# One normalisation moved to VectorE, one key tile fewer for VectorE, three accumulator banks in the tail of an attention-plus-MLP block on one core

## The chip, the cores and the metric

The kernel runs on one core of one Trainium2 chip. The metric is the device time of one execution in microseconds, and several executions of one kernel are summed up by their median. The profiled execution has a time of its own and a span, from its first to its last instruction. The engines are TensorE (PE; its weight loads are PEld), VectorE (DVE), ScalarE (ACT), GpSimd (POOL) and SyncE (SP), which issues most DMAs.

## The reference, cut to what matters

```python
mod = (_silu(c) @ w_mod).reshape(c.shape[0], 6, 1, -1)
sa, ca, ga, sb, cb, gb = mod[:, 0..5]
h = _layernorm(x) * (1 + ca) + sa                     # x: 2048 tokens x 512
q, k, v = split(h @ wqkv)                             # 32 heads of 16
p = softmax(q @ k.T / 4); o = p @ v
x = x + ga * (o @ wo)
h = _layernorm(x) * (1 + cb) + sb
x = x + gb * (gelu(h @ w1 + b1) @ w2 + b2)            # 512 -> 1376 -> 512
```

## The kernel before

**Attention.** The 2048 queries are four blocks of 512. The heads are worked in 32 groups `qi` of four; the 2048 keys are 16 tiles of 128. For a group and a key tile TensorE makes four 128x512 score tiles (line 944), one for each row `r` of four heads. Two ways lead from the scores to probabilities:

- ScalarE takes the exponential of two score tiles at a time out of PSUM into `pA` or `pB` (line 1300).
- VectorE turns scores into 16-bit integers that, read as half floats, are a rough power of two (line 1371, four passes for one group and key tile). Three shifted copies of the result follow, made by VectorE (line 1342) or GpSimd (line 1348), and TensorE weights the four copies with `VE` and three scaled variants `VV`.

TensorE multiplies the probabilities with the values (line 1108). The key tiles that VectorE may take are listed in `DKT`. In the last query block the last four groups are "halved": each covers four head pairs for 256 tokens, so that the first 256 tokens (the first half) are done with attention earlier than the second half, and one line-1108 product becomes two of 256 columns.

**Order.** A planner runs while the program is built: it simulates the engines with fixed costs and appends instructions to each engine's queue in the simulated order. The engines then run their queues in order, with semaphores. `d_next` decides when VectorE opens a new key tile; in the last group it opens none when fewer than `D_END` of the group's key tiles are unclaimed ("row tiles left"). Tasks such as the norm have an engine, and for the planner a cost.

**The first half.** When its attention is done, `add_half` puts out: the product with `W_o` and the residual (line 789, VectorE), the layer norm's statistics (lines 281, 286, VectorE), the root `ln_root` (lines 291, 292, GpSimd), the norm `n2` (line 804, two tiles of 128 tokens, on the engine that `N2_ENG` names), and two DMA transposes into `ha` (line 513, on SP's queue behind the eight `rb` loads of line 1474). A task of GpSimd can carry a further dependency, by which it starts after the VectorE instruction that preceded it in the plan.

**The tail.** `last_tail` is written by hand and comes after the last group's products. Its own chain is the second half's: copy the accumulator (`o`, line 1639), pick out the denominators (line 1644, fp32 products), reciprocal and spreading (lines 1646 to 1651), normalise (line 1655), `W_z` product, statistics, root on GpSimd, norm on VectorE and ScalarE (lines 1671, 1670), transposes (line 1676), and up products of the second half. Between these steps stands work of the first half, drawn by `gap(n)` from the generator `fillers`: eleven `up_one` (four 128x256 products of `ha` into a PSUM bank, then a gelu on ScalarE, line 1620), each followed by two yields, and then 22 products of the second MLP matrix, eleven for each of two token tiles, into the banks `dA[0]` and `dA[1]`. `GAPS` says how many yields each gap takes.

At the end VectorE adds the residual to the two first-half tiles (`out_add`, line 1690) and then makes `range_flag` (lines 1712 to 1720), a check on the denominators. Its result `bad` is an operand of a 1x1 TensorE product (line 1696), behind which the last 33 MLP products of the second half are queued.

Of the kernel before, what the change touches and what calls it, by code (L numbers as in the profile page):

```python
# [52 lines left out]
PE, AC, DV, PO = range(4)  # L53
# [44 lines left out]
TIE = True  # L98
SEARCH = None
NARROW = False  # L100
GAPS = (4, 2, 2, 17, 2, 3)
NHQ = 4
N2_ENG = PO
NHC = NC - NHQ // 2
MMH = 0.25
SP_DH = (0.5, 1.75)
# [1 line left out]
U2_GATE = (1.7, 4.6)  # L108
OUT2_GATE = (4.6, 7.2)
LOAD_AT = (0, 3)  # L110
D_END = 5
BULK_LEFT = 8
Z_GATE = 0.6

# [49 lines left out]
def adaln_block(ctx: ExitStack, tc: tile.TileContext, A_x, A_wqkv, A_wo, B_x, B_w1, B_b1, B_w2, B_b2,  # L164
# [81 lines left out]
    def bank(i):  # L246
        return PS[:, i, :]
# [41 lines left out]
    def ln_root(mv, n):  # L289
        rs = small.tile([P, 4], FP32, name="rs")  # L290
        nc.gpsimd.tensor_scalar(out=rs[:, 0:n], in0=mv[:, 0:n, 1], scalar1=EPS, scalar2=None, op0=ALU.add)  # L291
        nc.gpsimd.tensor_tensor(out=rs[:, 0:n], in0=rs[:, 0:n], in1=mhalf[:, 0:n], op=ALU.pow)
        return rs
# [36 lines left out]
    def copy(eng, dst, src):  # L330
        if eng == AC:
            nc.scalar.copy(out=dst, in_=src)
        else:
            nc.vector.tensor_copy(out=dst, in_=src)
# [150 lines left out]
    def task(*a, **k):  # L485
        tasks.append(Task(*a, **k))
# [201 lines left out]
    def plain(ps, lhsT, rhs, start, stop):  # L688
        nc.tensor.matmul(out=ps, lhsT=lhsT, rhs=rhs, start=start, stop=stop)  # L689

    def up_mm(ps, h2, fc, j, cs=slice(0, 512), mm=plain):
        mm(ps, late["W_1"][:, j, fc * P:(fc + 1) * P], h2[:, j, cs], j == 0, j == NC - 1)
# [91 lines left out]
    def add_half():  # L784
# [16 lines left out]
        def n2(tt):  # L801
            hn.append(otp.tile([P, 512], BF16, name="OT"))
            eng = nc.vector if N2_ENG == DV else nc.gpsimd
            eng.tensor_scalar(out=hn[tt], in0=xa[:, tt, :], scalar1=XL["mv"][:, tt, 0:1],  # L804
                                    scalar2=XL["rs"][:, tt:tt + 1], op0=ALU.subtract, op1=ALU.mult)

        for tt in range(2):
            task(("n2", b, tt), XA_AT, [("r2", b)] + [("n2", b, 0)] * tt, N2_ENG, 0.36 if N2_ENG == DV else 0.55,
                 lambda tt=tt: n2(tt))
# [8 lines left out]
    def ua(fc):  # L818
        return hT[:, fc // 3, 768 + 256 * (fc % 3):1024 + 256 * (fc % 3)]
# [147 lines left out]
    def d_next(now, avoid):  # L967
        if dcur[0] is None:
# [5 lines left out]
            left = sum(1 for i in range(st["ap"], len(order)) if order[i] not in owner) if aq >= NQ - 1 else 99  # L974
            if left < D_END:
                return None
# [625 lines left out]
    def last_tail():  # L1602
# [13 lines left out]
        def up_one(fc, k, half):  # L1616
            ps = bank(k)[:, 0:256]
            for j in range(NC):
                up_mm(ps, h2 if half else ha, fc, j, hB if half else hA)
            nc.scalar.activation(out=uG[:, fc, hB] if half else ua(fc), in_=ps, func=ACT.Gelu_apprx_tanh, bias=b1c[:, fc:fc + 1],  # L1620
                                 scale=1.0)

        def fillers():
            for fc in range(NFC):
                up_one(fc, (kw, dA[1])[fc % 2], 0)
                for _ in range(2):
                    yield
            for tt in range(2):
                for fc in range(NFC):
                    plain(bank(dA[tt]), ua(fc)[:, tt * P:(tt + 1) * P], late["W_2"][:, fc, :], fc == 0, fc == NFC - 1)  # L1630
                    yield

        gen = fillers()

        def gap(n):
            for _ in range(n):
                next(gen, None)

        nc.vector.tensor_copy(out=o, in_=bank(kO))
        nc.scalar.activation(out=onec, in_=onec, func=ACT.Gelu_apprx_tanh)  # L1640
        gap(GAPS[0])
        cols = [slice(P * i, P * i + P) for i in range(4)]
# [3 lines left out]
        nc.vector.reciprocal(out=rt.rearrange("p t r -> p (t r)"), in_=bank(kd)[:, 0:16])  # L1646
        gap(GAPS[1])
        for i in (0, 2, 1, 3):
            nc.vector.tensor_copy(out=rx[:, cols[i]].rearrange("p (r e) -> p r e", e=32),
                                  in_=rt[:, i, :].unsqueeze(2).to_broadcast([P, 4, 32]))  # L1650
            nc.tensor.matmul(out=bank(kr)[:, cols[i]], lhsT=rx[:, cols[i]], rhs=ident32, start=True, stop=True)
        gap(GAPS[2])
        for t in range(2):
# [10 lines left out]
        rs = ln_root(mv, 2)  # L1664
        gap(GAPS[3])
        nb = small.tile([P, 2], FP32, name="nb")
# [12 lines left out]
        copy(DV, h2[:, 2:4, hB], both[1][:, 2:4, :])  # L1679
        gap(GAPS[4])  # L1680
        for t in range(2):
            copy(DV, xr[:, 2 + t, :], bank(pz[t]))
        for fc in range(NFC):
            up_one(fc, (kO, kw, kd, kr)[fc % 4], 1)
            if fc == GAPS[5]:
                gap(99)

        def out_add(tt, k):
            obs[tt] = tl2.tile([P, D], BF16, name="ob")
# [138 lines left out]

    scr_d1 = scr.tile([4, 512], FP32, name="d1")
    last_tail()  # L1830
    att.close()
    general_path()
# [35 lines left out]
```

## Time and profile before

| what | value |
|---|---|
| median of 3 runs | 761.46 us (759.64 to 761.6) |
| the profiled execution's own time | 760.97 us |
| its span | 759.2 us |
| mean granted TensorE clock | 0.991 |
| busy: PE, ACT, DVE, POOL | 97%, 95%, 90%, 56% |
| last ScalarE exponential starts | 719.46 us |
| last TensorE instruction group starts | 754.35 us |

All times inside the profile are microseconds from the start of the span. The page's second part cuts the span into 40 slices of 19 us; each digit is tenths. The chain of waits names, for the work that ended last, what released each step. "x28" stands for 28 instructions of one kind in a row; their starts are real, and ends of matmuls are modelled, so neighbours overlap by a fraction of a microsecond. In the windows view, PEclk is the TensorE clock that was granted, as a share of full speed.

### The profile page before, as it was taken

The numbers are of one execution on the slowest core, as the hardware profiler recorded it, in microseconds if no ns is written. First come the engines' busy times: TensorE is split into PE (matmuls) and PEld (weight loads), VectorE is DVE, ScalarE is ACT, GpSimd is POOL, SyncE is SP. The second block draws the span as 40 slices with busy tenths as digits, with TensorE's granted clock in tenths as the row PEclk, the third lists the DMA queues.
The fourth block names the chain that finished last, engine by engine and source line by source line (L and its number), as shares of the span: only waits on it lengthen the run. The fifth ranks groups of instructions, "written<-read, shape, count | busy, mean of one in ns | idle before, by whom it ended". The sixth has DMA issues, their size and how long they took to land.

```text
span 759.2 us, 22066 instructions
## 1 busy us (share of the span) xinstructions
PE 737.3 (97%) x9027; PEld 241.3 (32%) x9030; DVE 679.7 (90%) x1189; ACT 719.7 (95%) x777; POOL 421.7 (56%) x266
## 2 busy tenths in 40 slices
PE   7999999999999999999999999999999999999977
PEld 3322322232333222222222222222222223344445
DVE  5958999999999899899999999999999989898823
ACT  3999999999999999999999999999999999999933
POOL 3202556566675655766565667756666465355720
PEclk9999999999999999999999999999999999999979
DMA  9410100021110110000101100000100200011000
GB/s 317 112 18 2 25 10 17 7 91 38 44 50 10 30 24 19 6 21 22 44 17 24 31 10 17 11 15 24 46 16 10 44 8 16 7 41 31 26 16 31
DMA packets 41964, 25.60 MB, mean 34 GB/s; under 512 B 26705, under 2 KB 37010, under 8 KB 41858
## 3 DMA queue, kind: packets, MB, share of 16 engines
q1 hardware_dynamic: 41042, 23.02, 11.7%
q8 instruction: 72, 1.18, 0.6%
q10 hardware_dynamic: 816, 1.12, 0.4%
q14 instruction: 34, 0.28, 0.1%
HBM read 16.59 MB, written 2.61 MB: 25 GB/s over the span
## 4 chain that ended last, share of the span: by engine, by line
PE 44%; ACT 43%; issue 8%; POOL 2%; DVE 1%; DMA 1%; POOLq 0%; ACTq 0%
ACT pB L1300 21%; ACT pA L1300 21%; PE PS L1108 15%; PE PS L944 15%; PE PS L254 10%; PE PS L689 2%; ACT uG L749 1%; POOL t L1348 1%; POOL OT L804 1%; DMA xb<-in_A_x_dram 0%; DVE st L281 0%; PE PS L1125 0%; DVE t L1371 0%; ACT uG L1620 0%; ACT L1300 0%
## 5 line engine op out<-in xcount | busy, mean ns | idle before, releaser
L1348 POOL TENSOR_SCALAR t<-t 128x2048 int16<-128x2048 int16 x188 | 355.7, 1901 | 257.6 <-DVE t L1342 149.7
L1300 ACT ACTIVATE pA<-PS 128x1024 bf16<-128x1024 f32 x368 | 395.1, 1074 | 3.4 <-PE PS L944 3.3
L1300 ACT ACTIVATE pB<-PS 128x1024 bf16<-128x1024 f32 x368 | 395.2, 1074 | 0.2
L1371 DVE TENSOR_SCALAR t<-PS 128x512 int16<-128x512 f32 x576 | 372.6, 682 | 25.0 <-PE PS L944 21.0
L944 PE MATMUL PS<-qm,kT 32*128 32x512 bf16 x2048 | 306.8, 383 | 6.5 <-ACT pA L1300 2.7
L1108 PE MATMUL PS<-t,VV 128*32 128x512 f16 (+1 forms) x1968 | 228.6, 358 | 2.5 <-POOL t L1348 1.4
L944 PEld LDWEIGHTS <-kT 32*128 32x128 bf16 x2048 | 85.1, 91 | 288.6 <-issue 285.5
L1342 DVE TENSOR_SCALAR t<-t 128x2048 int16<-128x2048 int16 x244 | 174.2, 743 | 0.5
L1108 PE MATMUL PS<-pA,VE 128*32 128x512 bf16 (+1 forms) x824 | 170.2, 362 | 0.0
L1108 PE MATMUL PS<-pB,VE 128*32 128x512 bf16 (+1 forms) x824 | 165.7, 362 | 0.0
L1108 PE MATMUL PS<-t,VE 128*32 128x512 f16 (+1 forms) x656 | 134.6, 358 | 0.2 <-DVE t L1371 0.2
L1108 PEld LDWEIGHTS <-VE 128*32 128x32 bf16 x2304 | 70.0, 94 | 76.6 <-issue 70.3
L1108 PEld LDWEIGHTS <-VV 128*32 128x32 bf16 x1968 | 65.4, 95 | 55.6 <-issue 51.1
L254 PE MATMUL PS<-h2T,W 128*32 128x512 bf16 x528 | 42.7, 383 | 0.0
L254 PE MATMUL PS<-W,uG 128*32 128x512 bf16 x528 | 41.3, 383 | 0.0
L1125 PE MATMUL PS<-kT,zeros 128*32 128x512 bf16 x284 | 27.4, 383 | 0.0
L341 DVE TENSOR_SCALAR qm<-PS,qmask 128x512 bf16<-128x512 f32 x32 | 22.5, 743 | 4.6 <-PE PS L254 4.6
L740 DVE TENSOR_SCALAR uG<-PS,b1c 128x512 bf16<-128x512 f32 x33 | 24.5, 744 | 1.1 <-PE PS L254 1.1
L291 POOL TENSOR_SCALAR rs<-mv 128x4 f32<-128x4 f32 (+1 forms) x10 | 4.3, 433 | 37.4 <-DVE mv L286 37.3
L1486 POOL TENSOR_TENSOR OT<-o_sb,rb 128x512 bf16<-128x512 f32 (+1 forms) x17 | 20.0, 1179 | 9.0 <-DVE t L1342 7.6
L254 PE MATMUL PS<-hT,W_k 128*32 128x512 bf16 x256 | 21.3, 394 | 0.9 <-DVE hT L324 0.9
L254 PE MATMUL PS<-hT,W_q 128*32 128x512 bf16 x256 | 21.4, 399 | 0.0
(142 smaller groups left out, 385.2 us busy)
## 6 DMA issues: line engine op xcount, KB each, us to landing
rb<-d SPq DMA_DIRECT2D x112, 32.0 KB
W_m<-in_w_mod_dram SPq DMA_DIRECT2D x2, 1024.0 KB
out_dram<-ob SPq DMA_DIRECT2D x15, 128.0 KB
o_sb<-o SPq DMA_DIRECT2D x56, 32.0 KB
xb<-in_A_x_dram SPq DMA_DIRECT2D x3, 512.0 KB
xr<-in_A_x_dram SPq DMA_DIRECT2D x3, 512.0 KB
W<-in_B_w_dram SPq DMA_DIRECT2D x4, 344.0 KB
W<-in_B_w_dram SPq DMA_DIRECT2D x5, 256.0 KB
```

What stands on the lines that cost most here:

```text
L254: nc.tensor.matmul(out=ps[32 * g:32 * g + 32, :], lhsT=lhsT[:, 32 * g:32 * g + 32], rhs=rhs, start=start, stop=stop)
L341: nc.vector.tensor_scalar(out=qm[(b, ch)][:, par, :], in0=ps, scalar1=qmask[:, par:par + 1], scalar2=None, op0=ALU.mult)
L689: nc.tensor.matmul(out=ps, lhsT=lhsT, rhs=rhs, start=start, stop=stop)
L740: nc.vector.tensor_scalar(out=X["u"][:, fc, :], in0=bank(ps), scalar1=late["b1c"][:, fc:fc + 1], scalar2=None, op0=ALU.add)
L944: nc.tensor.matmul(out=dst, lhsT=kT[rows, ch, kt * P:(kt + 1) * P], rhs=rhs, start=True, stop=True)
L1108: nc.tensor.matmul(out=bank(O[qi])[32 * r:32 * r + 32, cs], lhsT=w, rhs=rhs[:, cs], start=(n == 1 and not halved(qi)), stop=last and (pr = ...
L1125: nc.tensor.matmul(out=bank(O[qi])[32 * r:32 * r + 32, :], lhsT=zeros[:, 0:32], rhs=kT[:, 0, 0:512], start=False, stop=False)
L1300: nc.scalar.activation(out=t[:, 0:n, :], in_=PS[:, b0:b0 + n, :], func=ACT.Exp, scale=math.log(2.0) / STEP)
L1342: nc.vector.tensor_scalar(out=t16[:, rs, :], in0=d["tile"][:, rs, :], scalar1=float(MJ[j]), scalar2=None, op0=ALU.add)
L1348: nc.gpsimd.tensor_scalar(out=t16[:, rs, :], in0=d["tile"][:, rs, :], scalar1=1.0, scalar2=float(MJ[j]), op0=ALU.mult, op1=ALU.add)
L1371: nc.vector.tensor_scalar(out=d["tile"][:, r:r + n, :], in0=PS[:, i:i + n, :], scalar1=T_BIAS, scalar2=0.0, op0=ALU.add, op1=ALU.max)
L1486: nc.gpsimd.tensor_tensor(out=ot[:, 0:w], in0=o[:, 0:w], in1=rb[:, 0:w], op=ALU.mult)
```

## The change

`N2_ENG` becomes VectorE, so the two `n2` tiles run there. `D_END` becomes 6: VectorE opens no new key tile in the last group once fewer than six are unclaimed. The first half's up products rotate over three banks in place of two. And the last gap, which emptied the generator behind the fourth up product of the second half, now takes 13 yields there; what is left comes behind the eleventh.

```diff
-GAPS = (4, 2, 2, 17, 2, 3)
+GAPS = (4, 2, 2, 17, 2, 3, 13)
-N2_ENG = PO
+N2_ENG = DV
-D_END = 5
+D_END = 6
...
         def fillers():
             for fc in range(NFC):
-                up_one(fc, (kw, dA[1])[fc % 2], 0)
+                up_one(fc, (kw, dA[1], dA[0])[fc % 3], 0)
                 for _ in range(2):
                     yield
...
         for fc in range(NFC):
             up_one(fc, (kO, kw, kd, kr)[fc % 4], 1)
             if fc == GAPS[5]:
-                gap(99)
+                gap(GAPS[6])
+        gap(99)
```

The lines behind the change are one line further down in the changed kernel (line 1690 becomes 1691, and so on).

## The prediction

> **What bounds the kernel now.** The page comes first. Its row of the granted clock has full speed everywhere but in one slice, the last but one:
>
> ```profile
> PEclk9999999999999999999999999999999999999979
> ```
>
> So the 720 us ahead of the tail are steady, and the tail is read by itself. The order of instructions in the changed program is that of before up to about 711 us, so all that can change lies behind that point. The chain of waits over the last 39 us:
>
> ```profile
> 720.17 4.15 POOL OT L804 x2
> ...
> 724.33 2.43 DMA hT<-OT
> ...
> 726.80 1.89 PE PS L689 x8
> 728.69 1.50 PE PS L1644 x8
> 730.19 0.87 PE PS L689 x4
> 731.07 1.99 PE PS L1651 x8
> 733.05 2.92 PE PS L689 x12
> ...
> 736.00 0.48 ACT hT L1620
> ...
> 737.16 0.48 ACT hT L1620
> ...
> 739.85 0.78 ACT OT L1670
> ...
> 741.69 6.03 PE PS L689 x37
> ```
>
> GpSimd's two norms (line 804) and the transposes behind them end last, then the tail runs on TensorE, with ScalarE's gelus between. The view of who waited for whom prices the head of this chain, and TensorE's timeline shows what stood before it:
>
> ```profile
> PE PS L689 <- DMA hT<-OT: 4.3, 1, 4.3
> ```
>
> ```profile
> 722.11 0.40 PE L1108 MATMUL PS<-pB,VE 128*32 128x256 bf16 x4
> ```
>
> TensorE ended attention at 722.5 and stood 4.3 us until the first half's `ha` had landed. The price is more than 4.3 us, as the windows show. The columns are: the stretch, its length, busy us of PE, PEld, DVE, ACT and POOL, granted clock, DMA share and GB/s. The cuts lie on one grid of 3.41 us, placed so that each stretch has a single clock:
>
> ```profile
> 8.25:11.66 3.41, 2.23 (x48) 1.71 (x48) 1.67 (x6) 0.83 (x2) 0.68 (x3) 1.00 1.09 350
> 11.66:15.08 3.42, 3.17 (x32) 1.30 (x28) 1.05 (x10) 1.20 (x2) 0.00 (x0) 0.50 1.09 348
> ...
> 721.63:725.04 3.41, 0.88 (x7) 0.17 (x5) 0.69 (x1) 0.47 (x2) 2.67 (x2) 1.00 0.20 38
> 725.04:728.45 3.41, 1.65 (x8) 1.22 (x9) 0.00 (x0) 0.47 (x1) 0.00 (x0) 0.50 0.21 41
> 728.45:731.87 3.42, 3.42 (x18) 2.91 (x17) 0.89 (x5) 0.95 (x2) 0.00 (x0) 0.50 0.02 2
> 731.87:735.29 3.42, 3.42 (x14) 1.95 (x14) 1.23 (x3) 0.47 (x1) 0.00 (x0) 0.50 0.00 0
> ```
>
> The clock was halved behind each window in which TensorE did little, and came back behind a window of dense products. Because of the wait, the tail ran at half clock until 735.29.
>
> **Part 1, the norm on VectorE.** It removes the two GpSimd norms of the chain (4.15 us) and their place behind another GpSimd task. What they need stands in VectorE's and GpSimd's timelines, and what one costs on VectorE in the same operation on the same shape at line 296:
>
> ```profile
> 711.12 0.67 DVE L789 TENSOR_TENSOR hT<-PS,hT 128x512 bf16<-128x512 f32 x1
> ...
> 715.07 4.28 DVE L1342 TENSOR_SCALAR t<-t 128x2048 int16<-128x2048 int16 x7
> ```
>
> ```profile
> 715.24 1.13 POOL L291 TENSOR_SCALAR rs<-mv 128x2 f32<-128x2 f32 x1 [0.64 <-DVE mv L286]
> 716.46 1.12 POOL L292 TENSOR_TENSOR rs<-rs,mhalf 128x2 f32<-128x2 f32 x1
> ```
>
> ```profile
> L296 DVE TENSOR_SCALAR uG<-xr,mv,rs x12: 327/411/415, 260.2 to 588.5; 128x512 bf16<-128x512 bf16 x12
> ```
>
> In the new order VectorE does, after line 789 (done 711.8), the second statistics, one shift and the two aggregates (no passes of a last key tile stand between any more; two and a half steps at the shifts' 4.28 / 7 = 0.61, so by 713.3), then three shifts, the first norm, one shift, the second norm. GpSimd's root takes 2.3 us beside VectorE's shifts, so it is ready by 715.6, and the second norm is done by 715.6 + 0.41 + 0.61 + 0.41 = 717.0. On VectorE the norms queue ahead of the copy of line 1639 alone, which waits for TensorE anyway. SP is at the eight `rb` loads until 716.3:
>
> ```profile
> 712.12 4.20 SPq L1474 DMA_DIRECT2D rb<-d x8
> ```
>
> Before, the landing came 2.4 us after the second norm (724.33 to 726.76). So `ha` lands near 719.5, or 721 with everything as slow as before (root at 717.6). Either is ahead of the end of attention: the wait goes to nothing, and what is late next is attention itself.
>
> **Part 2, one key tile fewer for VectorE.** Four passes and three shifts leave VectorE and GpSimd, 24 products leave TensorE (four filling ones come in), and ScalarE gets two more exponentials, which are the bound there:
>
> ```profile
> 718.56 1.12 ACT L1300 ACTIVATE pA<-PS 128x1024 bf16<-128x1024 f32 x1
> 719.46 1.13 ACT L1300 ACTIVATE pB<-PS 128x1024 bf16<-128x1024 f32 x1
> 720.61 1.28 ACT L1640 ACT_TABLE_LOAD   x1
> ```
>
> Starts are 0.90 apart, so the last ends at 720.59 + 1.80 = 722.4. The last four products follow (0.40 and a semaphore): TensorE is at the tail at 722.9, 0.4 later than before. The fewer products on TensorE (0 to 0.8 us) I take at 0, since ScalarE ends last. The table load now ends at 723.7, beside TensorE's first fillers. So the restart moves from 726.80 to 722.9: **-3.9 us**.
>
> **The clock that comes with it.** With no wait, the clock stays full if the tail's first microseconds count as busy. Four rows then halve: 1.89, 1.50, 1.99 and the `W_z` products,
>
> ```profile
> 733.74 1.78 PE L689 MATMUL PS<-W_z,OT 128*128 128x512 bf16 x4
> 735.36 4.08 PE L689 MATMUL PS<-hT,W 128*128 128x256 bf16 x28
> ```
>
> 7.16 / 2 = 3.6; a little of it turns into waiting for VectorE's steps between them. I take **-3.4 us**, between 0 (clock halved as before) and -3.6.
>
> **Part 3, three banks.** With two banks two gelus took 1.16 us (736.00 to 737.16), since the product waits until the gelu of two before has read its bank. With three the bound is ScalarE, 0.45 each:
>
> ```profile
> 742.33 1.79 ACT L1620 ACTIVATE uG<-PS,b1c 128x256 bf16<-128x256 f32 x4 [0.69 <-PE PS L689]
> ```
>
> Before, line 1670 came 4.49 us after the seven products' start at 735.36 (739.85). Now it is 0.64 for the first product and seven gelus of 0.44: 3.7. That is **-0.75 us**, between 0 and -1.0. Bank `dA[0]` is later the first MLP accumulator; its gelu is two before the last and done by then.
>
> **Part 4, the split gap.** The 17 MLP products before become 13, and four move behind the 28 up products. In TensorE's time that is nothing. But the second `out_add` waits for the last of them, `range_flag` is queued behind it on VectorE, and TensorE's next instruction waits for `bad`. Before, 28 up products hid that:
>
> ```profile
> 743.44 3.83 PE L689 MATMUL PS<-W,hT 128*128 128x512 bf16 x17
> 747.11 3.22 PE L689 MATMUL PS<-h2T,W 128*128 128x256 bf16 x28
> 750.45 0.16 PE L1696 MATMUL PS<-onec,bad 128*1 128x1 bf16 x1
> 750.77 0.59 PE L689 MATMUL PS<-W,uG 128*128 128x512 bf16 x2 [0.16 <-issue]
> ```
>
> ```profile
> 747.30 0.69 DVE L1690 TENSOR_TENSOR ob<-PS,hT 128x512 bf16<-128x512 f32 x1 [1.68 <-PE PS L689]
> ...
> 749.92 0.06 DVE L1720 MEMSET onec<- 128x1 bf16 x1
> ```
>
> From the last MLP product (its end modelled at 747.27) to `onec` done (749.98) are 2.71 us, and from there to the first product behind line 1696 0.79. With nothing left to cover it TensorE stands 3.50 us where it stood 0.44: **+3.1 us**.
>
> The sum against this execution's own 760.97: -3.9 - 3.4 - 0.75 + 3.1 = -4.95, that is 756.0. Then the clock once more: 3.5 us of standing fill most of a 3.41 us window wherever the grid lies. The window 721.63 to 725.04 had 0.88 busy and was followed by half clock, so I take one such window as likely. The rest of the run is 5.0 us of TensorE work, by a last row of the chain:
>
> ```profile
> 750.77 4.96 PE PS L689 x34
> ```
>
> One halved window of dense work, like that from 11.66 to 15.08, costs at most 1.7, less what is still standing: **+1.55**. Bounds are 0 and +5.0 (halved to the end). Forecast: 757.5. The three runs shown have their median 0.5 above the profiled execution and spread over 2 us; I leave the forecast at the profiled level.
>
> **A rule beside this.** The window from 8.25 to 11.66 had 2.23 us of busy time, in small products, and half clock followed. The Trainium skill ("TensorE: Matmul & The Clock Gate", Part 1) states that the free-running window is about 3.4 us and that the clock falls after at least one idle window. If "idle" means wholly idle, the rule would hardly let the clock fall in a 3.5 us wait, and it would be the first rival below; these rows speak against that reading.
>
> **The rivals.**
> First, the clock holds through the flag's wait: 756.0. For it: a stand of 3.50 us can lie astride two windows of 3.41, each then about half busy. Against it: the row with 0.88 busy. Chance 0.25.
> Second, the tail's first microseconds, with the small products of line 1644 and pauses for VectorE, count as idle too. One halved window there costs half of 3.41, 757.5 + 1.7 = 759.2; two cost 760.9. For it: the row 8.25 to 11.66. Against it: by the halved rows 2.1 of the first 3.4 us are wide products (0.95 and 0.44 of fillers, most of 1.0 of line 1651). Chance 0.11, about no change.
> Third, slower, by one mechanism, the clock gate: only windows busy by more than about two thirds count. Then the chain gets none of the 3.4, and after the flag's wait the clock stays halved to the end: 760.97 - 3.9 - 0.75 + 3.1 + 5.0 = 764.4. Against it: the clock came back after one window at 15.08. Chance 0.07.
> Fourth, the change doesn't bring `ha` forward: GpSimd's root starves beside VectorE's shifts, and the restart stays at 726.80. Then nothing pays but the banks: 760.97 - 0.75 + 3.1 + 1.55 = 764.9. The norm would have to be 5 us later than worked out; the root's two rows show 2.3 us beside seven shifts. Chance 0.05.
>
> **How the numbers follow.** The forecast has 0.52, its own range being 756.2 to 758.9. No change is what lies within 0.3%, 2.3 us, about what a measurement of this kernel can tell from none. The forecast but 0.04, and the first rival, are faster: 0.73. That 0.04 and the second rival are the same: 0.15. The third and fourth are slower: 0.12. The range reaches from the first rival with its banks' and chain's far bounds (less 1.0, and 0.5 for the restart: 754.5) to the second rival's far end, 761.0; it leaves out about 0.14.
>
> **What would show it.** In the profile after: line 804 on VectorE near 716, `ha` landed before 720; the last exponential near 721.3; TensorE at the fillers near 723 with full clock; gelus 0.45 apart; line 1670's activation near 732; TensorE standing about 3.5 us ahead of line 1697, released by VectorE, and half clock for up to 3.4 us behind it. It is wrong if TensorE does not stand there, if the restart is not before 724, or if the clock falls between 723 and 732.

## The result and the profile after

The changed kernel takes 756.35 us (median of four runs, 755.61 to 757.42) against 761.51 us of the kernel before (759.64 to 761.6). The ratio is 0.9939, its 95% interval 0.9918 to 0.9961: faster by about 5 us. The profiled execution took 755.64 us, with a span of 753.9 us and a mean granted clock of 0.997. The page's row of the granted clock has its one weak slice at the very end now, no longer one before it:

```profile
PEclk9999999999999999999999999999999999999998
```

The timelines of the changed kernel answer the prediction's steps; the columns are start, length, engine, line, operation, and in brackets the idle time in front and what ended it. First VectorE with the norm (line 804), which waits for GpSimd's root, and SP with the issue of the two transposes that land `ha`:

```profile
711.92 1.86 DVE L1342 TENSOR_SCALAR t<-t 128x2048 int16<-128x2048 int16 x3
714.39 0.41 DVE L804 TENSOR_SCALAR OT<-hT,mv,rs 128x512 bf16<-128x512 bf16 x1 [0.61 <-POOL rs L292]
714.72 0.69 DVE L1342 TENSOR_SCALAR t<-t 128x2048 int16<-128x2048 int16 x1
715.33 0.41 DVE L804 TENSOR_SCALAR OT<-hT,mv,rs 128x512 bf16<-128x512 bf16 x1
```

```profile
714.88 3.63 SPq L513 DMA_TRANSPOSE hT<-OT  x2
```

This row is the issue in SP's queue, and the transfers land later: before, the same row ended at 722.26 + 3.26 = 725.52 and `ha` landed at 726.76. Here the semaphore of the second transpose is complete at 719.64 in the trace, nearly two microseconds ahead of TensorE's need. TensorE's timeline in the tail shows that it no longer waits for `ha`, and where it waits instead:

```profile
721.26 0.29 PE L1108 MATMUL PS<-pB,VE 128*32 128x256 bf16 x2
721.48 1.05 PE L689 MATMUL PS<-hT,W 128*128 128x256 bf16 x8
...
726.77 3.22 PE L689 MATMUL PS<-hT,W 128*128 128x256 bf16 x28
...
736.79 3.22 PE L689 MATMUL PS<-h2T,W 128*128 128x256 bf16 x28
739.85 1.03 PE L689 MATMUL PS<-W,hT 128*128 128x512 bf16 x4
743.65 0.16 PE L1697 MATMUL PS<-onec,bad 128*1 128x1 bf16 x1 [2.78 <-DVE onec L1721]
743.75 3.94 PE L689 MATMUL PS<-W,uG 128*128 128x512 bf16 x11
```

VectorE, in the same stretch, starts the second `out_add` when the last of the four products is done, and the range check stands in its queue behind it:

```profile
740.91 0.69 DVE L1691 TENSOR_TENSOR ob<-PS,hT 128x512 bf16<-128x512 f32 x1 [4.74 <-PE PS L689]
741.52 0.42 DVE L1713 TENSOR_SCALAR rb<-dall 128x512 f32<-128x512 f32 x1
...
743.52 0.06 DVE L1721 MEMSET onec<- 128x1 bf16 x1
```

The view of who waited for whom has at its head the new wait, where it had the one for the DMA before:

```profile
PE PS L1697 <- DVE onec L1721: 2.8, 1, 2.8
```

The windows (columns as in the prediction) say what the clock made of that wait, and that the start of the run has no halved window this time; from 11.66 to 15.08 it had one before. But for the first, they lie on this execution's grid:

```profile
11.66:15.08 3.42, 2.51 (x41) 1.05 (x40) 2.29 (x12) 1.41 (x3) 0.00 (x0) 1.00 1.09 348
...
722.71:726.12 3.41, 2.95 (x24) 2.22 (x24) 1.59 (x7) 1.43 (x4) 0.00 (x0) 1.00 0.03 5
...
739.80:743.21 3.41, 1.07 (x6) 0.33 (x4) 2.23 (x4) 0.72 (x2) 0.00 (x0) 1.00 0.11 38
743.21:746.62 3.41, 2.97 (x8) 1.11 (x9) 0.48 (x4) 0.00 (x0) 0.00 (x0) 0.50 0.00 0
746.62:750.03 3.41, 3.41 (x28) 2.64 (x27) 1.12 (x2) 0.00 (x0) 0.00 (x0) 1.00 0.13 43
```

Because of that first row every later time of the two traces is shifted. The MLP gelu of line 749, long before anything that the change touches, measures the shift; the chain of waits of before, then that of after:

```profile
650.01 4.90 ACT uG L749
```

```profile
648.61 4.90 ACT uG L749
```

That is 1.40 us, in no part of the change. With it taken off, TensorE restarts at 721.48 + 1.40 = 722.88 on the scale of before, where it restarted at 726.80. So two numbers sum up a kernel from here on: the **restart**, TensorE's first filler on the scale of before (by line 749), and the **tail**, from that filler to the end of the span. Before: 726.80 and 759.2 - 726.80 = 32.40. After: 722.88 and 753.9 - 721.48 = 32.42. The restart came 3.92 us earlier, and the tail is as long as before, although its clock was full and its gelus ran on three banks: the split gap took back all that these two gave. The span is given to 0.1 us, so a tail is good to 0.05 us, and a difference of two tails of less than 0.1 us says nothing.

### The profile page after: what moved, and what is told of

Read it like the earlier page. It is cut to its first block, busy times and chain, and to the rows that moved or that the text cites. A ratio compares the mean times of both kernels' runs of the same rounds, so it can differ in the third digit from the quotient of the medians.

```text
span 753.9 us, 22023 instructions
## 1 busy us (share of the span) xinstructions
PE 734.1 (97%) x9010; PEld 238.2 (32%) x9010; DVE 676.5 (90%) x1185; ACT 721.2 (96%) x779; POOL 415.6 (55%) x263
## 4 chain that ended last, share of the span: by engine, by line
ACT 50%; PE 38%; issue 9%; DVE 1%; POOL 1%; DMA 0%; DVEq 0%; ACTq 0%; POOLq 0%
ACT pB L1300 24%; ACT pA L1300 24%; PE PS L1108 13%; PE PS L944 13%; PE PS L254 8%; PE PS L689 3%; ACT uG L749 1%; POOL t L1348 1%; DMA xb<-in_A_x_dram 0%; PE PS L1125 0%; ACT hT L1620 0%; ACT L1300 0%; DVE st L281 0%; PE PS L311 0%; ACT hT L321 0%
```

## The experiments

Each kernel was timed in five rounds beside the kernel before on the same chip. Here they are together; the restart and the tail are read in each kernel's profile, and "full clock" is the median of those of its runs whose mean granted clock was 1.000.

| kernel | median us | ratio | 95% interval | restart | tail | full clock |
|---|---|---|---|---|---|---|
| before | 760.72, 759.70, 760.63 on three chips | 1 | | 726.80 | 32.40 | none |
| after | 756.35 | 0.9939 | 0.9918 to 0.9961 | 722.88 | 32.42 | none |
| norm alone | 753.22 | 0.9901 | 0.9877 to 0.9925 | 723.03 | 29.03 | 752.6 |
| tiles alone | 753.30 | 0.9907 | 0.9882 to 0.9933 | 722.88 | 29.14 | 752.8 |
| banks alone | 760.65 | 0.9995 | 0.9980 to 1.0010 | as before | 31.12 | none |
| split gap alone | 765.04 | 1.0064 | 1.0041 to 1.0087 | as before | 34.19 | none |
| all but the gap | 752.74 | 0.9905 | 0.9887 to 0.9923 | 722.87 | 28.16 | 751.5 |
| flag early | 751.47 | 0.9893 | 0.9876 to 0.9909 | 722.88 | 28.03 | 751.4 |
| flag, kept busy | 754.76 | 0.9942 | 0.9926 to 0.9959 | 722.87 | 30.80 | 754.2 |
| wait, kept busy | 757.56 | 0.9968 | 0.9955 to 0.9980 | 726.79 | 29.08 | 756.4 |
| early flag and busy start | 754.40 | 0.9918 | 0.9899 to 0.9936 | 722.88 | 28.08 | 751.6 |
| early flag, five row tiles | 754.27 | 0.9902 | 0.9885 to 0.9918 | 723.04 | 27.88 | 751.4 |

The theory ahead of them was the prediction's: the wait for `ha` costs itself and the clock behind it, and the split gap takes part of that back by a wait of its own. Its rivals were that one part alone does it all, that the banks matter more than they seem, and that the half-clock window behind the flag has another cause than TensorE's idleness.

**The norm alone.** Before, with one constant changed.

```diff
-N2_ENG = PO
+N2_ENG = DV
```

> The kernel before with the two norms on VectorE and nothing else. My theory (each of the first two parts is enough by itself): the root is ready at 717.6 as before, the norms end near 719.0 on VectorE, `ha` lands near 721.5, ahead of the end of attention (722.5), so the wait of 4.3 us goes and the clock stays full: 4.2 + 3.4 less, about 754. Rival (the norm's engine alone is too late, the missing key tile is what does it): 1 to 3 us less, and TensorE still waits for the transposes. Second rival (only the wait counts, the clock stays halved in the tail): about 757.

It gains nearly 1%, more than the whole change: the two intervals just touch, and the tails are 29.03 and 32.42 us. The timelines of VectorE, SP and TensorE (1.74 us late against the scale of before, by line 749 at 651.75) show the norm 1.8 us later than in the kernel after on a common scale, behind the passes of the last key tile, and the transposes still in time:

```profile
719.28 0.41 DVE L804 TENSOR_SCALAR OT<-hT,mv,rs 128x512 bf16<-128x512 bf16 x1 [0.61 <-POOL rs L292]
...
720.53 1.89 DVE L1342 TENSOR_SCALAR t<-t 128x2048 int16<-128x2048 int16 x3
```

```profile
719.72 2.64 SPq L513 DMA_TRANSPOSE hT<-OT  x2
```

```profile
722.48 0.41 PE L1108 MATMUL PS<-t,VV 128*32 128x256 f16 x8 [0.19 <-DVE t L1342]
...
723.26 0.81 PE L689 MATMUL PS<-W_o,OT 128*128 128x512 bf16 x3
...
724.77 1.04 PE L689 MATMUL PS<-hT,W 128*128 128x256 bf16 x8
```

`ha` lands at 723.72 by the trace's semaphores, a microsecond ahead of the first filler at 724.77. What ends last now are VectorE's three shifts behind the norm, done at 720.53 + 1.89 = 722.42: the chain of waits goes from them to the products of line 1108 at 722.48 and then along TensorE, without a pause, to the fillers. On VectorE these shifts stand behind both norms, and the first norm waits 0.61 us for the root. So this part alone takes the wait for `ha` away, and attention's end is what is late next.

**The tiles alone.**

```diff
-D_END = 5
+D_END = 6
```

> The kernel before with no new key tile for VectorE below six, norms still on GpSimd. My theory: root ready near 715.5, two norms of 2.07 us on GpSimd to 719.7, `ha` lands near 722.1, just ahead of the later end of attention (722.9): about 754, as much as the norm alone. Rival (the norm on GpSimd stays late, as its place behind the other GpSimd task is the cause): 1 to 3 us less than before. Then ScalarE's two exponentials more would be a loss of 0.4 to 1.8 with nothing for it.

The same gain again, with the norm still on GpSimd. GpSimd's timeline shows why:

```profile
714.68 1.12 POOL L292 TENSOR_TENSOR rs<-rs,mhalf 128x2 f32<-128x2 f32 x1
715.95 4.15 POOL L804 TENSOR_SCALAR OT<-hT,mv,rs 128x512 bf16<-128x512 bf16 x2
720.07 0.73 POOL L1486 TENSOR_TENSOR OT<-o_sb,rb 128x256 bf16<-128x256 f32 x1
```

The norm costs its 4.15 us as before but starts at 715.95 where it started at 720.17. Two things moved it. Without the last key tile VectorE has the statistics done sooner, so the root is done at 715.80, where it was done at 717.58. And in this kernel's order the norm stands ahead of GpSimd's other task, line 1486; before it stood behind that task, which waited for a shift of VectorE until 719.43. The rival was that the norm would stay late because of its place behind that task. It didn't stay late, but the place changed together with the key tile, and of the 4.2 us only 1.8 go with the earlier root.

The two parts aren't additive. Each brings `ha` in before attention ends, with the tiles alone only just (landed at 722.73, first filler at 722.86, a scale that is 0.02 us off that of before), and then attention's end bounds: restart 723.03 with the norm alone, 722.88 with the tiles alone, 722.88 with both. Restart and tail together are the same within what a tail is good for, 752.06 and 752.02.

**The banks alone.**

```diff
-                up_one(fc, (kw, dA[1])[fc % 2], 0)
+                up_one(fc, (kw, dA[1], dA[0])[fc % 3], 0)
```

> The kernel before with three banks for the first half's products. My theory: the seven products from 735.36 on are at full clock and gain 0.75 us; 760.7. Rival (another step ends last there, so nothing): 761.5.

The timelines of TensorE and ScalarE:

```profile
734.83 3.22 PE L689 MATMUL PS<-hT,W 128*128 128x256 bf16 x28
```

```profile
735.47 3.09 ACT L1620 ACTIVATE hT<-PS,b1c 128x256 bf16<-128x256 f32 x7 [1.28 <-PE PS L689]
738.46 0.77 ACT L1670 ACTIVATE OT<-PS,nb,rs 128x512 bf16<-128x512 f32 x1
```

Line 1670 comes 738.46 - 734.83 = 3.63 us behind the first of the 28 products, where it was 4.49: 0.86 us shorter. The mechanism is there, with gelus 0.44 apart. (The tail is 1.3 us shorter, but 0.3 of that is another position on the grid: the halved clock ends 0.6 us sooner behind the restart, and the 28 products follow it by 8.25 us in place of 8.56.) The runs can't tell the kernel from before (interval 0.9980 to 1.0010), nor theory from rival: the 0.75 us would be 0.9990.

**The split gap alone.** Part 4 on top of before, where the wait for `ha` remains.

```diff
-GAPS = (4, 2, 2, 17, 2, 3)
+GAPS = (4, 2, 2, 17, 2, 3, 13)
...
-                gap(99)
+                gap(GAPS[6])
+        gap(99)
```

> The kernel before with the split gap: 13 yields behind the fourth product, the rest behind the eleventh. My theory: TensorE stands 2.9 to 3.5 us for the flag where it stood 0.4, and about one window of half clock follows (1.5 us): 765 to 766. Rival (the flag's wait was hidden by something else and the stand in the changed kernel has another cause): 761.5.

It costs 0.64%, about 4.9 us. The profiled execution is not a typical one: at 761.44 us and a mean granted clock of 0.996 it is the fastest of twelve, and the others go up to 770.91 us at 0.980 to 0.993. It has the same stand of TensorE as the kernel after, with another outcome; TensorE's timeline, then the windows on its grid:

```profile
751.01 0.16 PE L1697 MATMUL PS<-onec,bad 128*1 128x1 bf16 x1 [2.78 <-DVE onec L1721]
751.11 2.55 PE L689 MATMUL PS<-W,uG 128*128 128x512 bf16 x11
```

```profile
746.49:749.90 3.41, 1.75 (x13) 0.94 (x10) 1.59 (x3) 1.40 (x4) 0.00 (x0) 1.00 0.01 5
749.90:753.32 3.42, 2.31 (x12) 1.10 (x13) 1.12 (x5) 0.00 (x0) 0.00 (x0) 1.00 0.10 34
```

The stand of 2.78 us lies across two windows here, 1.75 and 2.31 us busy, and the clock stays full: the eleven products take 2.55 us, where the kernel after needed 3.94. The Trainium skill ("TensorE: Matmul & The Clock Gate", Part 1) says that the window of about 3.4 us runs free and doesn't reset when a kernel starts. The two traces agree: one wait, two positions on the grid, two clocks. The tail of this execution is only 1.8 us longer than before, since the wait for `ha` also fell otherwise here and halved the clock for two windows (726.01 to 732.84), where before it was three. Where the slower executions lost their clock is not seen; the median, 4.3 us above that of before, is what the wait with the clock behind it was expected to cost.

**All but the gap.** The changed kernel with part 4 undone: the first three diffs above on top of before.

> The changed kernel without the split gap (the last gap empties the generator behind the fourth product, as before). My theory: the stand of 2.8 us for the flag and the half clock behind it (1.6 us) go: 4 us less than the changed kernel, about 752. Rival (the clock does not hang on that stand): 2.4 us less, 754. Second rival (another wait takes the place): no less than 756.

TensorE's timeline has no wait in front of the flag's product:

```profile
739.02 3.22 PE L689 MATMUL PS<-h2T,W 128*128 128x256 bf16 x28
742.36 0.16 PE L1696 MATMUL PS<-onec,bad 128*1 128x1 bf16 x1
742.46 2.55 PE L689 MATMUL PS<-W,uG 128*128 128x512 bf16 x11
```

The tail is 28.16 us, against 29.03 with the norm alone (the banks' 0.87) and 32.42 after. So the split gap costs 32.42 - 28.16 = 4.26 us where the other parts are in and the clock falls behind the wait, as it did in the profile of after.

**The flag early.** The changed kernel, split gap and all, but the range check is queued on VectorE ahead of the two `out_add`s; the denominators that it reads are complete long before.

```diff
         for t in range(2):
             copy(DV, xr[:, 2 + t, :], bank(pz[t]))
+        bad, onec_, fl = range_flag()
...
         for tt in range(2):
             out_add(tt, dA[tt])
-        bad, onec_, fl = range_flag()
```

> The changed kernel with the split gap, but the five VectorE instructions of the range check queued ahead of the first half's additions. My theory: the flag is ready long before, so TensorE stands under 0.5 us and the gap's place costs nothing: about 752, as without the split. Rival (it is the second addition and its bank that TensorE waits for): no change, 756.

VectorE does the check in idle time, and TensorE runs through:

```profile
736.56 0.06 DVE L1721 MEMSET onec<- 128x1 bf16 x1
```

```profile
741.03 1.03 PE L689 MATMUL PS<-W,hT 128*128 128x512 bf16 x4
741.99 0.16 PE L1697 MATMUL PS<-onec,bad 128*1 128x1 bf16 x1
742.09 2.55 PE L689 MATMUL PS<-W,uG 128*128 128x512 bf16 x11
```

The tail is 28.03 us: all that the split gap cost was its wait and the clock behind it. This is the version with the lowest median, 0.9893 of before. The split itself, made harmless, gains nothing that the tails or the runs show (28.03 against 28.16; 751.4 against 751.5 at full clock).

**The flag's wait, kept busy.** The changed kernel with twelve products of zeros put on TensorE between the last MLP product and the flag's. The wait stays as it is.

```diff
         bad, onec_, fl = range_flag()
+        warm(12, kw)
```

> The changed kernel with twelve products of zeros (0.22 us each) queued ahead of the flag's product, into a bank that is free: TensorE works where it stood, the wait for the flag is as long. My theory (low activity halves the clock): clock full to the end, 1.6 us less, about 754.7. Rival (the clock falls for another reason): 756.3, half clock behind the flag as before.

The timeline of TensorE:

```profile
740.83 2.75 PE L259 MATMUL PS<-zeros 128*128 128x512 bf16 x12
743.77 0.16 PE L1698 MATMUL PS<-onec,bad 128*1 128x1 bf16 x1 [0.19 <-DVE onec L1722]
743.87 2.55 PE L689 MATMUL PS<-W,uG 128*128 128x512 bf16 x11
```

And the windows, at the same place on the grid as in the kernel after:

```profile
739.80:743.21 3.41, 3.41 (x20) 1.60 (x17) 2.11 (x4) 0.84 (x2) 0.00 (x0) 1.00 0.11 38
743.21:746.62 3.41, 3.22 (x18) 1.50 (x17) 0.77 (x5) 0.00 (x0) 0.00 (x0) 1.00 0.00 0
```

The flag's product still waits for VectorE, but the products behind it run at full clock. The tail is 30.80 us, between the 28.16 without the wait and the 32.42 with it idle: about 2.6 us are the wait, about 1.6 us the clock behind it. It was idleness that cost the clock.

**The wait for `ha`, kept busy.** Before, with eighteen products of zeros while TensorE waits for `ha`. This is the other half of the theory by itself: the wait stays, the clock should not fall.

```diff
         nc.scalar.activation(out=onec, in_=onec, func=ACT.Gelu_apprx_tanh)
+        warm(18, kw)
         gap(GAPS[0])
```

> The kernel before with eighteen products of zeros (3.9 us) queued where TensorE waits for the transposes: the wait is as long, but TensorE is busy. My theory: the clock stays full in the tail, 3.4 us less, about 758. Rival (the clock falls anyway, as the tail's small products count as idle): 761.5, half clock from about 729 on.

TensorE's timeline and the windows in which the kernel before was 0.88 us busy and then at half clock:

```profile
722.36 4.06 PE L259 MATMUL PS<-zeros 128*128 128x512 bf16 x18
726.72 1.05 PE L689 MATMUL PS<-hT,W 128*128 128x256 bf16 x8 [0.30 <-DMA hT<-OT]
```

```profile
721.63:725.04 3.41, 3.41 (x20) 1.39 (x18) 0.69 (x1) 0.39 (x2) 2.59 (x2) 1.00 0.20 38
725.04:728.45 3.41, 3.11 (x24) 2.06 (x23) 0.00 (x0) 0.85 (x2) 0.00 (x0) 1.00 0.21 41
```

The fillers start as late as before and run at full clock. The tail shrinks from 32.40 to 29.08, as short as with the norm alone, and the kernel is 0.32% faster though it does more work. Of what the norm or the tiles alone bring, the wait is thus 3.8 to 3.9 us and the clock 3.3 in these traces.

**Early flag and busy start.** The flag-early kernel with seven products of zeros in the first 12 us (three behind the first norm, four ahead of the modulation's copy), against the halved window near 11.66.

> The changed kernel with the range check queued early (as in the run before) and, at the start of the program, seven products of zeros more where TensorE waits for VectorE: three between the two pairs of transposes, four ahead of the first key product. My theory (low activity in the first 12 us gives one window of half clock in about half of the runs, 1.2 us each): the runs lie together at the lower level, 751.4. Rival (the dip at the start has another cause): as before two levels, 751.4 and 752.6. Second rival (the products delay the first key product): 752 or more.

The six runs fall into pairs: 751.56 and 751.40 at a mean clock of 1.000 and 0.999, 754.53 and 754.27 at 0.995, 755.88 and 756.11 at 0.993. They didn't come together, so the start is not the only place where a run can lose the clock. Only one run was profiled, one at full clock, so where the others lost theirs is not seen.

**Early flag, five row tiles.** The flag-early kernel with the tile part undone.

```diff
-D_END = 6
+D_END = 5
```

> The changed kernel with the range check queued early, but with VectorE's last key tile as before (D_END 5): norms on VectorE, three banks, split gap, early check. My theory (the norm alone brings `ha` in time, and the two exponentials more and the later VectorE work cost each other's gain): within 0.5 us of the run with the tile left out, about 751.5. Rival (the two exponentials more cost their 1.8 us): 750. Second rival (without the tile left out the norm is late): 754 or more.

The runs at 754.3 to 754.5 had a clock of 0.995, the one at full clock took 751.37. The profiled execution, one of those at 0.995, lost its clock near 234 us, far from anything the change touches. Restart and tail together are 750.92, and 750.91 for the flag-early kernel: with the norm on VectorE, the key tile that part 2 takes away from it is worth nothing that can be seen.

## Why the prediction was right

**The restart, -3.9 us.** Right, to 0.02 us: 722.9 was forecast, 722.88 measured. On the scale of before the second norm was done at 715.33 + 0.41 + 1.40 = 717.1 (forecast 717.0). `ha` landed at 719.64 + 1.40 = 721.0, 1.5 us behind the 719.5 that were worked out and at the late bound of 721; it was still in time, so this cost nothing, though the sign "landed before 720" fails on this scale. That the figure fits so closely is in part luck. The working let ScalarE's last exponential set the end, and it did end as forecast (720.08 + 1.02 + 1.40 = 722.5; forecast 722.4), but TensorE's own products run without a pause from 717.41 to the restart in the trace of after, so two ends fall together. The price of part 2, 0.4 us of later attention, is not borne out: with the norm alone, without that part, the restart is 723.03, later still, because VectorE's last shifts stand behind the norm. And the working took the two parts as one cause; the runs show that either alone makes the wait go.

**The clock, -3.4 us.** Right in kind and size. From the restart to the 28 products the trace of after has 726.77 - 721.48 = 5.29 us, before it was 735.36 - 726.80 = 8.56: -3.27. Keeping the wait and taking its idleness away gave 3.32 of tail. The second rival, small products that count as idle, didn't occur: the window from 722.71 to 726.12 has 2.95 us busy, and the clock stays full until the flag's wait. The third, that only windows busy by two thirds count, falls with the split gap alone: a window 1.75 us busy, half of it, kept the clock. One reading under this term doesn't hold as written, that the clock "came back behind a window of dense products": in its own rows the window from 728.45 to 731.87 has TensorE busy throughout, and half clock follows.

**The banks, -0.75 us.** -0.86 measured (4.49 to 3.63), inside the bounds given.

**The flag's wait, +3.1 us.** The sign and the mechanism are as forecast, with VectorE's check as the releaser; this is the term that was mis-sized. TensorE stood 743.75 - 740.88 = 2.87 us (740.88 is the modelled end of the four products), not 3.50. The check itself was right: from the last MLP product's end to `onec` it is 743.58 - 740.88 = 2.70, forecast 2.71. The step that failed is "from there to the first product behind line 1696 0.79". In the trace of before `onec` had been ready since 749.98, while line 1696 had to wait until the 28 products ended at 750.33; so 0.35 us of the 0.79 were TensorE's own work and no latency. Another 0.22 are no time at all but a missing record. Eleven products belong behind line 1696; the trace of before has ten, the first of them 0.32 us behind that line, where every other trace has the first 0.10 us behind it. The page of before counts 9027 products for 9030 weight loads. From `onec` to the first product behind it are 743.75 - 743.58 = 0.17 us. With the missing product in its place TensorE stood 0.22 us before, not 0.44, and the net cost is 2.87 - 0.22 = 2.65, as the busy-wait kernel shows it.

**One half-clock window, +1.55.** Right for this trace: about 1.6 between the two tails. "Wherever the grid lies" was wrong: in the split gap alone the same stand fell across two windows and cost no clock. The first rival's mechanism is real, then, though neither the profile of after nor its four runs (at 755.6 twice, at 757.1 and 757.4) reached the 754.2 that go with it (the busy-wait kernel at full clock). By its number alone the median of 756.35 would speak for that rival, forecast at 756.0, rather than for 757.5; it is the trace that decides.

**The sum.** By the traces: -3.92 for the restart, -3.27 for the clock, -0.86 for the banks, and +4.15 from the end of TensorE's last work ahead of the flag to the end of the span (753.9 - 740.88 = 13.02, where it was 759.2 - 750.33 = 8.87) is -3.90; the forecast of 757.5 is -3.47 (its terms as written add up to -3.40), of which the split gap had 3.1 + 1.55 = 4.65. Of the 1.86 us between 757.5 and the profiled 755.64 some 0.4 are these terms, and 1.40 are the halved window at the start, which this execution didn't have. The prediction carried it over from the one execution of before as if it were part of the kernel, and its first reading, of "720 us ahead of the tail" as steady, passed it by: one halved window in a slice of 19 us leaves a clock of 0.91, which the page prints as 9. The windows that it showed itself have the 0.50.

## What to carry to other kernels

A wait on TensorE can have two prices, its length and the clock behind it, and the second can be nearly as large (3.3 us beside 3.8 for `ha`); filling the wait with useless products shows the second by itself. When several parts of a change remove the same wait, each may be enough, and the part that moves work in front of another wait can eat the gain: look for what is queued behind the moved work on each engine, as the range check was behind the `out_add`. Before a gap between two instructions is priced as a latency, look whether the engine was still busy in it, and whether all its records are there.

## What the runs showed of the hardware

**Where the clock's threshold lies.** Windows of 3.41 us with 0.88 and 1.07 us of wide products (26% and 31%) were followed by half clock; one with 1.75 us (51%) was not. The kernel with the banks alone narrows it from below: its window ahead of the wait for `ha` has 1.47 us (43%), and half clock follows.

```profile
720.81:724.22 3.41, 1.47 (x10) 0.41 (x8) 0.69 (x1) 1.06 (x2) 3.27 (x2) 1.00 0.20 38
```

The Trainium skill ("TensorE: Matmul & The Clock Gate", Part 1) has the clock fall after at least one idle window; here such a window need not be wholly idle.

**Half clock in dense work.** With the norm alone and with five row tiles, the clock was halved for some 7 us near 234 us, in the middle of attention, where the view of windows shows TensorE busy throughout. The kernel with the norm alone, on its grid:

```profile
230.77:234.18 3.41, 3.41 (x29) 1.81 (x27) 3.08 (x8) 3.41 (x5) 1.41 (x3) 1.00 0.03 5
234.18:237.59 3.41, 3.41 (x26) 0.58 (x22) 2.81 (x4) 2.88 (x3) 2.18 (x2) 0.50 0.14 39
```

The first of these windows holds 29 products, eight of them small ones in fp32 (line 661, 128x32), which start from 230.80 to 233.75. In the trace of after the same eight start from 230.48 to 233.43, and the grid parts them at 231.18, four and four; its clock stays full. All twelve traces fit: the window ahead of the loss holds eight of these products with the norm alone and seven with five row tiles, and no window of any other trace holds more than six. That the small ones count little as activity and the position on the grid decides is thus likely, but no experiment tried it.

**Levels of a kernel.** The runs of one kernel lie on levels that go with the mean granted clock: 752.5 to 752.6 at 1.000, 753.7 to 753.9 at 0.997 and 0.998, 755.6 at 0.995 with the norm alone. A halved window of 3.41 us takes 0.0023 off the mean clock and up to 1.7 us. The split gap alone spreads furthest, from 761.44 us at 0.996 to 770.91 at 0.980. A difference of one or two microseconds between two medians here may be no more than that, and it is why the table compares runs at full clock as well.
